# Delta-rule attention with a gated convolution: the 16-to-32 step in half as many products over 128 rows

## The chip, the cores and the metric

The kernel runs on one core of a Trainium2 chip. The metric is device microseconds of one execution. The core's engines have instruction queues of their own: TensorE (PE; its weight loads are listed as PEld), VectorE (DVE), ScalarE (ACT), GpSimd (POOL) and SyncE (SP). SP, ACT and POOL also issue DMA transfers (SPq, ACTq, POOLq).

## The reference

```python
def _attn_ref(q, k, v, beta) -> np.ndarray:
    B, H, S, D = q.shape          # 4, 8, 768, 48
    k_n = k / (np.linalg.norm(k, axis=-1, keepdims=True) + 1e-06)
    state = np.zeros((B, H, D, D), dtype=np.float32)
    y = np.zeros_like(q)
    for t in range(S):
        kt, vt, bt = (k_n[:, :, t], v[:, :, t], beta[:, :, t, None])
        y[:, :, t] = np.einsum('bhd,bhde->bhe', q[:, :, t], state)
        v_old = np.einsum('bhde,bhd->bhe', state, kt)
        state = state + bt[:, :, :, None] * np.einsum('bhd,bhe->bhde', kt, vt - v_old)
    return y.astype(np.float32)
```

Its output, 4 x 768 x 384, is the `x` of a gated convolution: `gate = sigmoid(conv of 5 taps over time)`, `out = (gate * (x @ w_val)) @ w_out`.

## The kernel before

**Tiling.** The 32 sequences (batch x head) are pairs: 16 pairs, one sequence in the upper and one in the lower 64 partitions. Time is cut into 12 chunks of 64 steps. Within a chunk the recurrence is solved as a triangular system; its inverse is built by doubling: blocks of 8 and 16 by small VectorE operations over all systems at once, then from 16 to 32 on TensorE (`m16`, `m32`), then from 32 to 64 (`lev1`, `lev2`). Two chunks make a group; the VectorE part runs once per group.

**A group's preparation.** `kq` (for the first group `kp` and `qp`) makes the Gram blocks of keys and queries; `kqevac` or `kpevac` takes them to GL on ScalarE, `kpfix` or the transfers `realign` shift half of the rows; `att` writes the masked query part. `trans_in` transposes to TL, `coef` and `newton` make the norms, `row`, `mergez8` and `merget8` the inverse of 16 x 16 blocks, `trans_out` writes them to XA (one half) and WB (the other). `gblocks` puts Gram blocks into G64 (transfer G<-GL), `wblocks` puts WB into W64: in group 0 by copies, later half by GpSimd copies and half by four transfers of SP (W<-WB). Per chunk, `m16` multiplies G64 with XA, `m16evac` takes it to YS, `m32` multiplies W64 with YS, `m32evac` takes it to XX; then `lev1`, `zevac`, `lev2`, `tevac`.

**A chunk's chain.** `e` (old state times keys), `eadd` on VectorE, `u`, `uevac`, `s` (new state, in SPS), `sevac`, and `y`; `stack` moves U and the masked part between halves of the partitions by transfers. `e` of the next chunk needs `sevac`.

**The convolution part.** Six segments of two chunks (the last cut in two): `conv`, `tap`, `sig`, `gate` on ScalarE and VectorE, `val` and `outp` on TensorE, `oevac`, and the store.

**Names in the trace of TensorE**: PB<-KQ is `kp`, `qp` or `kq`; PB<-XA,G `m16`; PB<-YS,W `m32`; PB<-XX,GL `lev1`; PB<-ZS,XX `lev2`; PB<-Y,KQ `e`; PB<-VT,XX `u`; SPS<-Y,KT and SPS<-US,KT `s`; PB<-KQ,Y `y`; PB<-X,WV `val`; PB<-WO,GT `outp`; SPS<-ZW `keep_warm`. Each product of the code is two instructions there.

**What sets the order.** Every operation is added to a plan with its reads and writes. The table ORDER is the order in which they are issued to the engines' queues; -1 in it is `keep_warm`, a product of zeros into an unused corner of SPS. BANKS gives each product group one of six PSUM banks. Each engine works its own part of ORDER strictly in turn.

The weights `w_val` and `w_out` come as double precision; `f64_0` to `f64_4`, `f64_low` and `f64_join` turn them into float32 on ScalarE, VectorE (lines 301 to 308) and GpSimd during the first third.

Of the kernel before, what the change touches and what calls it, by code (L numbers as in the profile page):

```python
# [16 lines left out]
C = 64  # L17
NCH = S // C
NG = NCH // 2
NP = 16  # L20
# [124 lines left out]
def kernel(  # L145
# [412 lines left out]
    def m32evac(ch, h):  # L558
        copy(A, XX[ch % NXX][:, HB * h:HB * h + HB, 32 * h:32 * h + 32], bank["m32", ch, h][:, 0:HB * 32].rearrange("p (j x) -> p j x", x=32))
# [499 lines left out]
```

## Time and profile before

| | |
|---|---|
| median of 3 runs | 322.74 us (318.75 to 323.77) |
| profiled execution | 322.35 us, its span 320.6 us |
| mean granted TensorE clock | 0.89 of full |
| busy: PE / DVE / ACT / POOL | 84% / 65% / 52% / 34% |
| bytes moved by DMA | 37.81 MB, 118 GB/s in the mean |

Busy shares are means over stages with different limits; matmuls are pipelined, so the start of one group and the start of the next tell more than a group's length. The granted clock has two levels, 1 (2.4 GHz) and 0.5 (1.2 GHz); a value between is a mean over a stretch.

### The profile page before, as it was taken

The numbers are of one execution on the slowest core, as the hardware profiler recorded it, in microseconds if no ns is written. First come the engines' busy times: TensorE is split into PE (matmuls) and PEld (weight loads), VectorE is DVE, ScalarE is ACT, GpSimd is POOL, SyncE is SP. The second block draws the span as 40 slices with busy tenths as digits, with TensorE's granted clock in tenths as the row PEclk, the third lists the DMA queues.
The fourth block names the chain that finished last, engine by engine and source line by source line (L and its number), as shares of the span: only waits on it lengthen the run. The fifth ranks groups of instructions, "written<-read, shape, count | busy, mean of one in ns | idle before, by whom it ended". The sixth has DMA issues, their size and how long they took to land.

```text
span 320.6 us, 16289 instructions
## 1 busy us (share of the span) xinstructions
PE 269.2 (84%) x7226; PEld 196.3 (61%) x7226; DVE 208.5 (65%) x461; ACT 166.0 (52%) x424; POOL 109.6 (34%) x255
## 2 busy tenths in 40 slices
PE   8204876688898988889897999698999997999996
PEld 4204865678654766567675565566665674766874
DVE  7989656598764879947737549756548800853580
ACT  3550457655447564468356384444276454576341
POOL 7313745448208527063262055180441140000000
PEclk9655597796679999999898999799999998999999
DMA  6999817833154748416763319564154132011123
GB/s 194 246 210 200 260 30 186 219 58 89 39 100 100 208 134 182 87 31 160 185 156 86 82 53 216 115 186 110 21 163 126 30 91 79 4 27 39 59 78 76
DMA packets 51398, 37.81 MB, mean 118 GB/s; under 512 B 33216, under 2 KB 44992, under 8 KB 51328
## 3 DMA queue, kind: packets, MB, share of 16 engines
q1 hardware_dynamic: 43392, 20.77, 27.6%
q0 software_dynamic: 4480, 13.64, 16.3%
q10 hardware_dynamic: 3456, 2.36, 3.2%
q8 instruction: 57, 0.93, 1.3%
q14 instruction: 13, 0.11, 0.1%
HBM read 22.92 MB, written 4.72 MB: 86 GB/s over the span
## 4 chain that ended last, share of the span: by engine, by line
PE 58%; DMA 11%; DVE 9%; ACT 7%; SPq 6%; issue 5%; ACTq 2%; POOL 2%; DVEq 0%
PE PB L243 28%; PE PB L705 13%; PE PB L715 13%; SPq L230 6%; DMA Y<-US 3%; PE SPS L243 2%; DMA G<-GL 2%; ACT XX L222 2%; ACTq L227 2%; DMA W<-WB 2%; ACT Y L222 2%; PE SPS L969 2%; DMA KQ<-AQ 1%; DMA X<-YSB 1%; DVE TLP L472 1%
## 5 line engine op out<-in xcount | busy, mean ns | idle before, releaser
L697 DVE SCALAR_TENSOR_TENSOR GT<-X,CW,GT 128x512 f32<-128x512 f32 (+1 forms) x84 | 56.3, 692 | 29.1 <-ACT GT L222 27.9
L705 PE MATMUL PB<-X,WV 128*128 128x512 f32 (+1 forms) x126 | 59.9, 596 | 2.6 <-ACT Y L222 1.6
L222 ACT ACTIVATE XX<-PB 32x256 f32<-32x256 f32 (+2 forms) x96 | 39.2, 427 | 30.1 <-PE PB L243 29.1
L715 PE MATMUL PB<-WO,GT 128*128 128x384 f32 x144 | 51.9, 499 | 0.6 <-ACT OS L222 0.6
L243 PE MATMUL PB<-KQ 48*64 48x128 f32 (+1 forms) x896 | 36.6, 313 | 17.0 <-DMA KQ<-in_qr_dram 5.9
L243 PEld LDWEIGHTS PB<-KQ 48*64 48x64 f32 x896 | 31.0, 173 | 24.2 <-ACT X L299 5.9
L715 PEld LDWEIGHTS PB<-WO,GT 128*128 128x128 f32 x144 | 25.7, 190 | 15.9 <-ACT OS L222 1.4
L705 PEld LDWEIGHTS PB<-X,WV 128*128 128x128 f32 x126 | 22.9, 201 | 15.0 <-issue 10.3
L222 ACT ACTIVATE GL<-PB 128x256 f32<-128x256 f32 (+1 forms) x44 | 16.0, 402 | 29.0 <-PE PB L243 17.7
L243 PE MATMUL PB<-KQ,Y 112*48 112x64 f32 (+2 forms) x768 | 27.5, 233 | 3.0 <-DMA Y<-US 2.5
L243 PEld LDWEIGHTS PB<-KQ,Y 112*48 112x48 f32 (+2 forms) x768 | 25.1, 133 | 7.3 <-issue 3.2
L222 ACT ACTIVATE Y<-PB 64x192 f32<-64x192 f32 x48 | 14.9, 322 | 19.7 <-PE PB L243 11.7
L411 DVE TENSOR_TENSOR KQ<-PB,MASK 64x256 f32<-64x256 f32 (+1 forms) x44 | 19.3, 443 | 7.3 <-ACT GL L222 6.5
L222 ACT ACTIVATE Y<-SPS 64x384 f32<-64x384 f32 (+1 forms) x44 | 20.4, 480 | 6.0 <-PE SPS L243 4.1
L709 DVE TENSOR_TENSOR GT<-PB,GT 128x512 f32<-128x512 f32 (+1 forms) x21 | 12.5, 609 | 14.6 <-ACT GT L701 8.0
L643 DVE TENSOR_TENSOR VT<-PB,VT 128x384 f32<-128x384 f32 x22 | 11.8, 554 | 15.6 <-issue 6.8
L243 PEld LDWEIGHTS PB<-VT,XX 64*64 64x64 f32 x768 | 13.8, 141 | 11.5 <-ACT XX L222 4.2
L243 PE MATMUL PB<-VT,XX 64*64 64x48 f32 x768 | 15.5, 227 | 6.1 <-DVE VT L643 2.5
L222 ACT ACTIVATE OS<-PB 128x384 f32<-128x384 f32 x24 | 11.5, 488 | 14.8 <-PE PB L715 9.6
L243 PE MATMUL PB<-XA,G 64*64 64x16 f32 x768 | 16.1, 223 | 3.3 <-DMA G<-GL 3.0
L591 POOL TENSOR_TENSOR VT<-VT,NRM 128x768 f32<-128x768 f32 x12 | 17.9, 1496 | 2.7 <-DMA VT<-in_vt_dram 1.2
L233 POOL DMA_DIRECT2D KQ<-in_qr_dram x16 | 8.9, 560 | 28.0 <-PE PB L243 28.0
(111 smaller groups left out, 459.6 us busy)
## 6 DMA issues: line engine op xcount, KB each, us to landing
out_dram<-OS SPq DMA_DIRECT2D x20, 192.0 KB, 2.6
KQ<-in_kf_dram POOLq DMA_DIRECT2D x16, 224.0 KB, 4.6
KQ<-AQ SPq DMA_DIRECT2D x24, 128.0 KB, 3.8
VT<-in_vt_dram POOLq DMA_DIRECT2D x16, 192.0 KB, 4.2
KT<-in_kt_dram POOLq DMA_DIRECT2D x16, 192.0 KB, 3.6
Y<-US ACTq DMA_DIRECT2D x24, 96.0 KB, 3.4
KQ<-in_qr_dram POOLq DMA_DIRECT2D x8, 256.0 KB, 5.0
KQ<-in_kf_dram SPq DMA_DIRECT2D x8, 224.0 KB, 4.5
```

The costliest lines, as they stand in the source:

```text
L222: A.activation(out=out, in_=in_, func=AF.Copy, **kw)
L227: A.dma_start(out=dst, in_=src)
L230: SP.dma_start(out=dst, in_=src)
L233: G.dma_start(out=dst, in_=src)
L243: PE.matmul(p, lhsT, rhs, start=start, stop=stop, tile_position=(row, col), skip_group_check=True)
L411: V.tensor_tensor(out=AQ[ch % NAQ][:, u:u + n] if v is None else R[ch % NR][r, v, u:u + n], in0=p[r], in1=MASK[h][r].unsqueeze(1).to_broad ...
L591: G.tensor_tensor(out=v, in0=v, in1=n.unsqueeze(3).to_broadcast([128, 2, HB, D]), op=ALU.mult)
L643: V.tensor_tensor(out=v, in0=bank["e", ch, h][:, 0:HB * D], in1=v, op=ALU.add)
L697: V.scalar_tensor_tensor(out=g, in0=xseg(sg, m, k), scalar=CW[:, m, k:k + 1], in1=g, op0=ALU.mult, op1=ALU.add)
L705: PE.matmul(bank["val", sg, m][:, 0:n], WV[:, k, 128 * m:128 * m + 128], xseg(sg, k, 4), start=k == 0, stop=k == NKT - 1)
L709: V.tensor_tensor(out=g, in0=bank["val", sg, m][:, 0:B * n].rearrange("p (b t) -> p b t", t=n), in1=g, op=ALU.mult)
L715: PE.matmul(bank["out", sg, i][:, 0:DM], gseg(sg)[:, k, w * i:w * i + w, :].rearrange("p b t -> p (b t)"), WO[:, k, :], start=k == 0, stop ...
```

## The change

`m16` and `m32` used products of 64 rows: two pairs' halves, each 64 x 64, and 32 products per chunk and step. Now one product covers both halves, 128 rows, with the moving tile block-diagonal: XA2 and YS hold the two halves' blocks side by side and zeros elsewhere. A chunk has 16 products for `m16` (32 moving columns, 16 before) and 16 for `m32` (64 moving columns, 32 before), each 128 x 64, and one PSUM bank per step instead of two. `spread` copies XA into XA2, one half on ScalarE, one on GpSimd; `m16evac` writes 64 partitions of 256 elements instead of 128 of 128, and YS holds one chunk instead of two. `wblocks` is a copy in all groups, four on ScalarE and four on GpSimd. `kpfix` goes half to ScalarE. Keys load rows 0 to 47 and 64 to 111 without the 16 rows between, in two transfers by row half instead of by head half; queries, from chunk 4 on, also without padding. ORDER and BANKS are new; ORDER holds 37 `keep_warm` (18 before).

```diff
 ORDER = [
-    13, 19, 29, 6, 23, 17, 14, 15, 28, 153, 154, 155, 1, 159, 156, 157, 158, 16, 31, 36, 40, 42, 41, 0, 30, 43, 235,
+    33, 34, 12, 6, 20, 16, 158, 32, 31, 17, 18, 35, 26, 27, -1, 36, 159, 46, 50, 47, 51, 240, 1, 19, 160, 161, 52, 49,
...
     G64 = one([128, NU, C], "G64")
     W64 = one([128, NU, C], "W64")
+    W5 = W64.rearrange("p (c j a) x -> p c j a x", c=2, a=2)
...
+    XA2 = one([128, NU, 32], "XA2")
     WB = one([128, NU, 16], "WB")
-    YS = one([128, NU, 32], "YS")
+    YS = one([128, NYS * NP, 64], "YS")
+    YS5 = YS.rearrange("p (c j a) x -> p c j a x", c=NYS, a=2)
...
     def kpfix(ch, h, a):
 
         q = 64 * a + 32 * (1 - h)
-        V.tensor_copy(out=GL[ch // 2 % 2][q:q + 32, h, ch % 2, :, 32 * h:32 * h + 32],
-                      in_=bank["kp", ch, h][q:q + 32].rearrange("p (j x) -> p j x", x=C)[:, :, 32 - 32 * h:64 - 32 * h])
+        copy(V if a else A, GL[ch // 2 % 2][q:q + 32, h, ch % 2, :, 32 * h:32 * h + 32],
+             bank["kp", ch, h][q:q + 32].rearrange("p (j x) -> p j x", x=C)[:, :, 32 - 32 * h:64 - 32 * h])
...
     def wblocks(g, q, h):
-        u, x, r = slice(NP * h, NP * h + NP), q % 64 + 16, (q + 64 * h) % 128
-        if g and h == 0:
-            load(W64[r + 16:r + 32, u, x:x + 16], WB[q + 16:q + 32, u])
-        else:
-            copy(G if h else A, W64[r:r + 32, u, x:x + 16], WB[q:q + 32, u])
+        x, a, r = q % 64 + 16, q // 64, q % 64 + 64 * h
+        t = WB.rearrange("p (h c j) x -> p h c j x", h=2, c=2)[:, h]
+        copy(G if h else A, W5[r:r + 32, :, :, a, x:x + 16], t[q:q + 32])
+
+    def spread(a):
+        r = slice(64 * a, 64 * a + 64)
+        copy(G if a else A, XA2[r, :, 16 * a:16 * a + 16], XA[r])
...
     def l_m16(ch, h):
-        p = bank["m16", ch, h]
-        for pp in range(HB * h, HB * h + HB):
-            for r in (0, 64):
-                to = 64 - r if h else r
-                yield p[to:to + 64, 16 * (pp % HB):16 * (pp % HB) + 16], G64[r:r + 64, unit(ch, pp), :], XA[r:r + 64, unit(ch, pp), :], r, to
+        p = bank["m16", ch]
+        for j in range(HB):
+            x = unit(ch, HB * h + j)
+            yield p[64 * h:64 * h + 64, 32 * j:32 * j + 32], G64[:, x, :], XA2[:, x, :], 0, 64 * h
...
     def m16evac(ch, h):
-        copy(A, YS.rearrange("p (h c j) x -> p h c j x", h=2, c=2)[:, h, ch % 2, :, 0:16],
-             bank["m16", ch, h][:, 0:HB * 16].rearrange("p (j x) -> p j x", x=16))
-
-    def l_m32(ch, h):
-        p = bank["m32", ch, h]
-        for pp in range(HB * h, HB * h + HB):
-            for r in (0, 64):
-                to = 64 - r if h else r
-                yield p[to:to + 64, 32 * (pp % HB):32 * (pp % HB) + 32], W64[r:r + 64, unit(ch, pp), :], YS[r:r + 64, unit(ch, pp), :], r, to
+        r, x = slice(64 * h, 64 * h + 64), 32 * h
+        copy(A, YS5[r, ch % NYS, :, :, x:x + 16].rearrange("p j a x -> p (j a) x"),
+             bank["m16", ch][r, 0:HB * 32].rearrange("p (s x) -> p s x", x=16))
+
+    def l_m32(ch, a):
+        p = bank["m32", ch]
+        for j in range(HB):
+            yield p[64 * a:64 * a + 64, C * j:C * j + C], W5[:, ch % 2, j, a, :], YS5[:, ch % NYS, j, a, :], 0, 64 * a
...
     def load_k(ch):
-        for h in range(2):
-            fetch(KF[ch % NKF][0:112, HB * h:HB * h + HB], kf[ch, :, HB * h:HB * h + HB], ch, [("KF", ch % NKF, h)], "LKF")
+        for f in range(2):
+            fetch(KF[ch % NKF][64 * f:64 * f + D], kf[ch, 64 * f:64 * f + D], ch, [("KF", ch % NKF, f)], "LKF")
 
     def load_q(ch):
         for v in range(2):
-            to = slice(0, 64) if v else slice(64, 112)
-            fetch(R[ch % NR][to, v], qr[ch, 1 - v, 0:to.stop - to.start], ch, [("R", ch % NR, "Q", v)], "LQR")
+            n = D if v == 0 or ch >= NR else C
+            to = 64 - 64 * v
+            fetch(R[ch % NR][to:to + n, v], qr[ch, 1 - v, 0:n], ch, [("R", ch % NR, "Q", v)], "LQR")
...
+        for a in range(2):
+            add("POOL" if a else "ACT", spread, (a,), r=["XA", "XA2z"], w=[("XA2", a)])
         for q in range(0, 128, 32):
             for h in range(2):
-                add("POOL" if h else "SP" if g else "ACT", wblocks, (g, q, h), r=["WB", "W64z"], w=[("W64", q, h)])
+                add("POOL" if h else "ACT", wblocks, (g, q, h), r=["WB", "W64z"], w=[("W64", q, h)])
```

The new ORDER at three places. First VectorE in the preparation of group 0, at the steps `row(5)` to the first of `mergez8`. L498 and L501 are the two steps of `row` (new: L503, L506), L308 and L301 steps of the weight conversion, L508 is `mergez8` (new: L513), L414 in the new order a mask (`att0`). Before:

```order
L498 TENSOR_TENSOR PR_85<-TT__84,TLP 128x100
L501 TENSOR_REDUCE TT__84<-PR_85 128x4x5
L498 TENSOR_TENSOR PR_85<-TT__84,TLP 128x144
L501 TENSOR_REDUCE TT__84<-PR_85 128x4x6
L308 TENSOR_SCALAR XX_79<-XX_79 128x384
L498 TENSOR_TENSOR PR_85<-TT__84,TLP 128x196
L301 TENSOR_SCALAR X_92<-X_92 128x384
L501 TENSOR_REDUCE TT__84<-PR_85 128x4x7
L508 TENSOR_TENSOR PR_86<-TLP,TT__84 128x128
```

Now:

```order
L503 TENSOR_TENSOR PR_85<-TT__84,TLP 128x100
L506 TENSOR_REDUCE TT__84<-PR_85 128x4x5
L503 TENSOR_TENSOR PR_85<-TT__84,TLP 128x144
L506 TENSOR_REDUCE TT__84<-PR_85 128x4x6
L414 TENSOR_TENSOR AQ_69<-PB_121,MASK_114 128x512
L503 TENSOR_TENSOR PR_85<-TT__84,TLP 128x196
L506 TENSOR_REDUCE TT__84<-PR_85 128x4x7
L513 TENSOR_TENSOR PR_85<-TLP,TT__84 128x256
```

The conversions have left this chain, and a mask of the second chunk has come in.

Second, SP's queue between the last G blocks of group 2 and the `realign` transfers of group 3 (GL<-GL); X<-YSB places `y` for the convolution, KQ<-AQ is the masked part. Before:

```order
L230 DMA X_92<-YSB_94 16x4x128 x4
L230 DMA W_75<-WB 16x16x16 x2
L230 DMA X_92<-YSB_94 16x4x128
L230 DMA W_75<-WB 16x16x16 x2
L230 DMA X_92<-YSB_94 16x4x128
L230 DMA KQ<-AQ_68 64x512
L230 DMA GL_73<-GL_73 32x16x32 x4
```

Now:

```order
L233 DMA G_74<-GL_72 16x32x16
L233 DMA X_93<-YSB_95 16x4x128 x5
L233 DMA KQ<-AQ_68 64x512
L233 DMA X_93<-YSB_95 16x4x128
L233 DMA KQ<-AQ_68 64x512
L233 DMA GL_73<-GL_73 32x16x32
```

The four W transfers are gone; the X transfers stay ahead of `realign`.

Third, ScalarE at the same group, around the evacuations of `m16` (YS<-PB). Before:

```order
L222 ACTIVATE OS_97<-PB_123 128x384
L222 ACTIVATE YS<-PB_124 128x8x16
L222 ACTIVATE YS<-PB_122 128x8x16
L222 ACTIVATE GT_96<-X_92,CW 128x512
L222 ACTIVATE YS<-PB_121 128x8x16
L222 ACTIVATE GL_73<-PB_124 128x256
```

Now:

```order
L225 ACTIVATE XA_89<-XA 64x32x16
L225 ACTIVATE GL_73<-PB_122 128x256
L225 ACTIVATE W_75<-WB 32x16x16 x3
L225 ACTIVATE YS<-PB_123 64x16x16
L225 ACTIVATE W_75<-WB 32x16x16
L225 ACTIVATE YS<-PB_123 64x16x16
L225 ACTIVATE GL_73<-PB_122 128x256
```

`spread` (XA_89<-XA) and four W copies have come in ahead of and between the evacuations of the first `m16`.

On TensorE, counted in the new ORDER: one `keep_warm` ahead of `kp`, 13 more before `m16` of chunk 2, one between there and the last output product, and 22 behind it (before: none, none, nine and nine). `kq` of chunk 2 and the first of chunk 3 stand ahead of the first `m16`; before, only one `kq` did.

## Rows read from the trace of the kernel before

**Rows 1.** Page, part 1: busy us, share of the span, instructions.

```profile
PE 269.2 (84%) x7226; PEld 196.3 (61%) x7226; DVE 208.5 (65%) x461; ACT 166.0 (52%) x424; POOL 109.6 (34%) x255
```

**Rows 2.** Windows: start:end us, length, busy us per engine, mean clock, DMA, GB/s.

```profile
74.40:93.70 19.30, 17.86 (x409) 13.27 (x401) 13.09 (x23) 8.01 (x23) 7.22 (x13) 0.65 0.30 61
93.70:139.20 45.50, 38.82 (x1250) 28.04 (x1250) 36.46 (x73) 26.51 (x69) 20.65 (x46) 1.00 0.55 133
...
234.90:277.90 43.00, 40.87 (x1084) 27.40 (x1083) 22.59 (x52) 23.59 (x60) 7.80 (x14) 0.96 0.30 85
277.90:316.20 38.30, 38.30 (x550) 26.75 (x549) 20.48 (x42) 20.09 (x52) 0.00 (x0) 1.00 0.18 49
316.20:320.60 4.40, 2.00 (x18) 1.80 (x17) 0.00 (x0) 0.49 (x1) 0.00 (x0) 1.00 0.36 87
```

**Rows 3.** Timeline of PE, 104 to 112 us: start, us, operation, idle before.

```profile
105.18 2.00 PE L243 MATMUL PB<-KQ,Y 112*48 112x64 f32 x64
107.11 1.15 PE L243 MATMUL PB<-Y,KQ 48*64 48x48 f32 x64
108.18 2.20 PE L715 MATMUL PB<-WO,GT 128*128 128x384 f32 x6
110.32 1.15 PE L243 MATMUL PB<-VT,XX 64*64 64x48 f32 x64
```

**Rows 4.** Timeline of PE, 256.8 to 267 us, the last `m16` and `m32`.

```profile
257.88 1.12 PE L243 MATMUL PB<-XA,G 64*64 64x16 f32 x64
258.93 2.20 PE L715 MATMUL PB<-WO,GT 128*128 128x384 f32 x6
...
264.25 2.07 PE L243 MATMUL PB<-YS,W 64*64 64x32 f32 x128
266.25 0.49 PE L969 MATMUL SPS<-ZW 128*128 128x128 f32 x2
```

**Rows 5.** Timeline of PE, 32 to 52 us.

```profile
32.73 2.15 PE L243 MATMUL PB<-XA,G 64*64 64x16 f32 x66 [2.96 <-DMA G<-GL]
...
40.24 1.56 PE L243 MATMUL PB<-YS,W 64*64 64x32 f32 x64
...
50.45 1.54 PE L243 MATMUL PB<-VT,XX 64*64 64x48 f32 x64 [2.40 <-POOL WV L315]
```

**Rows 6.** Timeline of DVE, 14 to 31 us.

```profile
19.30 0.36 DVE L301 TENSOR_SCALAR XX<-XX 128x384 f32<-128x384 f32 x1 [0.35 <-ACT XX L299]
...
23.33 1.17 DVE L301 TENSOR_SCALAR X<-X 128x384 f32<-128x384 f32 x1
...
30.02 1.03 DVE L529 STREAM_TRANSPOSE XA<-TT__84 128x512 f32<-128x512 f32 x1
```

**Rows 7.** Timeline of DVE, 50 to 62 us: `trans_in(1)` and `eadd(1)`.

```profile
50.89 1.95 DVE L472 STREAM_TRANSPOSE TLP<-GL 128x1024 f32<-128x1024 f32 x1 [1.62 <-DMA GL<-GL]
...
60.56 1.02 DVE L643 TENSOR_TENSOR VT<-PB,VT 128x384 f32<-128x384 f32 x2
```

**Rows 8.** Timeline of PE, 120 to 140 us: `m32(4)`.

```profile
130.30 1.45 PE L243 MATMUL PB<-YS,W 64*64 64x32 f32 x64 [1.13 <-DMA W<-WB]
```

**Rows 9.** Chain that ended last, in order of time: start, us, what.

```profile
25.23 7.36 DMA G<-GL
...
124.70 5.47 DMA W<-WB
...
310.38 5.81 PE PB L715 x18
316.19 2.01 PE SPS L969 x18
```

**Rows 10.** Groups by form, ACT: busy us, mean ns, idle before.

```profile
L222 ACT ACTIVATE YS<-PB 128x128 f32<-128x128 f32 x24 | 5.5, 275 | 10.8 <-PE PB L243 10.7
L222 ACT ACTIVATE G<-EYE 32x512 f32<-32x512 f32 x4 | 2.5, 622 | 0.1
L222 ACT ACTIVATE W<-WB 32x256 f32<-32x256 f32 x4 | 1.7, 414 | 0.1
```

More of the change, by code (lines that the diff above doesn't have):

```diff
@@ L40 @@
 ORDER = [
[70 rows of a table removed]
[71 rows of a table added]
 ]
 BANKS = (
-    "01234523304141500442511020300534334323130110105431405055345202510011041420301131321042332214511141053452133555"
-    "45532224313053154303513525103104253352541511124543243543444221043412240152103330525553324535313140114041423320"
-    "252414321331502"
+    "23014510000022325023435224012240141050343453245311325410222231131044101142535042321331244501111122215053522301"
+    "12430523403545203330510102425142405053524154231552402020333304052131030351451524220203400252521241350"
 )
@@ L169, in tiles @@
         return [one(shape, f"{name}{i}") for i in range(n)]
-    NKF, NR, NKTB, NVT, NAQ, NXX, NOS = 4, 4, 3, 3, 2, 4, 3
+    NKF, NR, NKTB, NVT, NAQ, NXX, NOS, NYS = 4, 4, 3, 3, 2, 4, 3, 1
     KQ = one([128, (NKF + 2 * NR) * NP * C], "KQ")
@@ L189 @@
     TT_ = one([128, 1056], "TT_")
-    PR = tiles(2, [128, 512], "PR")
+    PR = [one([128, 512 - 256 * i], f"PR{i}") for i in range(2)]
     ZT = one([128, 128], "ZT")
     XA = one([128, NU, 16], "XA")
+    XA2 = one([128, NU, 32], "XA2")
     WB = one([128, NU, 16], "WB")
-    YS = one([128, NU, 32], "YS")
+    YS = one([128, NYS * NP, 64], "YS")
+    YS5 = YS.rearrange("p (c j a) x -> p c j a x", c=NYS, a=2)
     XB = tiles(NX, [128, NKT, B, 2 * C + 4], "X")
@@ L558, in m32evac @@
     def m32evac(ch, h):
-        copy(A, XX[ch % NXX][:, HB * h:HB * h + HB, 32 * h:32 * h + 32], bank["m32", ch, h][:, 0:HB * 32].rearrange("p (j x) -> p j x", x=32))
+        copy(A, XX[ch % NXX][:, HB * h:HB * h + HB, 32 * h:32 * h + 32],
+             bank["m32", ch].rearrange("p (j h x) -> p j h x", h=2, x=32)[:, :, h])
     def l_lev(ch, h, n):
@@ L728 @@
             add("ACT", const_eye, (t[:, :, x:x + 16], 0, 16, r), r=["EYE"], w=[n + "z"])
-    add("ACT", const_eye, (YS[:, :, 16:32], 16, 16), r=["EYE"], w=["YSc"])
+    add("POOL", fill, (G, (XA2, 0.0)), w=["XA2z"], kind="zXA2")
+    add("POOL", fill, (G, (YS, 0.0)), w=["YSc"], kind="zYS")
+    for h in range(2):
+        r = slice(64 * h, 64 * h + 64)
+        add("ACT", const_eye, (YS[:, :, 32 * h + 16:32 * h + 32], 16, 16, r), r=["EYE"], w=["YSc"])
     add("ACT", const_eye, (ZS[:, :, 32:64], 0, 32), r=["EYE"], w=["ZSc"])
@@ L744 @@
     add("SP", load, (BE, beta), w=["BE"], kind="LB")
-    first = [("first", q) for q in range(0, 128, 32)]
     def load_k(ch):
-        for h in range(2):
-            fetch(KF[ch % NKF][0:112, HB * h:HB * h + HB], kf[ch, :, HB * h:HB * h + HB], ch, [("KF", ch % NKF, h)], "LKF")
+        for f in range(2):
+            fetch(KF[ch % NKF][64 * f:64 * f + D], kf[ch, 64 * f:64 * f + D], ch, [("KF", ch % NKF, f)], "LKF")
     def load_q(ch):
         for v in range(2):
-            to = slice(0, 64) if v else slice(64, 112)
-            fetch(R[ch % NR][to, v], qr[ch, 1 - v, 0:to.stop - to.start], ch, [("R", ch % NR, "Q", v)], "LQR")
+            n = D if v == 0 or ch >= NR else C
+            to = 64 - 64 * v
+            fetch(R[ch % NR][to:to + n, v], qr[ch, 1 - v, 0:n], ch, [("R", ch % NR, "Q", v)], "LQR")
     def q_of(ch):
@@ L782, in grams @@
                     for a in range(2):
-                        add("DVE", kpfix, (ch, h, a), r=[toks[h], *w], w=[("GD", gb, h, a, ch)], give=[toks[h]])
+                        add("DVE" if a else "ACT", kpfix, (ch, h, a), r=[toks[h], *w], w=[("GD", gb, h, a, ch)], give=[toks[h]])
             for ch in (2 * g, 2 * g + 1):
@@ L821, in prep @@
         for q in range(0, 128, 32):
-            add("SP", gblocks, (g, q), r=gl(0) + gl(1) + ["G64z"], w=[("G64", q)] + ([] if g else [("first", q)]))
+            add("SP", gblocks, (g, q), r=gl(0) + gl(1) + ["G64z"], w=[("G64", q)])
         plan_coef()
@@ L842, in prep @@
             x = ch % NXX
-            t1, t2 = ([(n, ch, h) for h in range(2)] for n in ("m16", "m32"))
-            add("PE", m16, (ch,), r=[("G64", q) for q in range(0, 128, 32)] + ["G64z", "XA"], w=t1, take=t1)
+            t1, t2 = ("m16", ch), ("m32", ch)
+            add("PE", m16, (ch,), r=[("G64", q) for q in range(0, 128, 32)] + ["G64z"] + [("XA2", a) for a in range(2)], w=[t1], take=[t1])
             for h in range(2):
-                add("ACT", m16evac, (ch, h), r=[t1[h]], w=[("YS", c, h)], give=[t1[h]])
-            add("PE", m32, (ch,), r=[("W64", q, h) for q in range(0, 128, 32) for h in range(2)] + ["W64z", "YSc"] + [("YS", c, h) for h in range(2)],
-                w=t2, take=t2)
+                add("ACT", m16evac, (ch, h), r=[t1, "YSc"], w=[("YS", ch % NYS, h)], give=[t1])
+            add("PE", m32, (ch,), r=[("W64", q, h) for q in range(0, 128, 32) for h in range(2)] + ["W64z", "YSc"] + [("YS", ch % NYS, h) for h in range(2)],
+                w=[t2], take=[t2])
             for h in range(2):
-                add("ACT", m32evac, (ch, h), r=[t2[h], ("XXz", x)], w=[("XX", x, "late", h)] + [("XX", x, h, a) for a in range(2)], give=[t2[h]])
+                add("ACT", m32evac, (ch, h), r=[t2, ("XXz", x)], w=[("XX", x, "late", h)] + [("XX", x, h, a) for a in range(2)], give=[t2])
             t1, t2 = ("lev", ch, 1), ("lev", ch, 2)
```

139 rows, old and new, of the table ORDER are left out of this document.

## Prediction

> **What bounds the kernel now.** I read the page first: TensorE is busy 84% of the span and no other engine comes near that [rows 1]. That share is a mean, so the second view is the busy time by stretch, with borders that I put at events of the work [rows 2]. From 93.70 on TensorE is busy 85% to 100% of every stretch, and from 277.90 to the last output product at 316.20 it never stops. Before 93.70 it is slow rather than idle: in 74.40 to 93.70 it is busy 17.86 of 19.30 us, but at a mean granted clock of 0.65. The clock has two levels, 1.2 and 2.4 GHz, so 70% of that stretch was at the lower one, and the lower one doubles a product's time: some 6.8 us of the 19.3.
>
> The third view is TensorE's timeline, read by the starts of neighbours, because durations overlap. At 2.4 GHz two `y` take 107.11 - 105.18 = 1.93 us, one `e` 1.07, one `u` 1.07 [rows 3], one `m16` 1.05, two `m32` 2.00 [rows 4]. A change of the tile's shape also costs: three output products in a row take 5.81 / 3 = 1.94 us each [rows 9], one that follows a product of another shape takes 110.32 - 108.18 = 2.14 [rows 3], so the switch is 0.20 us. With such unit costs and the order of the instructions, TensorE's work up to the last output product adds up to about 227 us of the 316; the other 89 us are waits and half clock. Two thirds of them lie ahead of chunk 3, where TensorE waits for VectorE's chain of small operations and for transfers. That is where an order can gain; behind it, only fewer or shorter products can.
>
> **Products.** The change takes 16 products of each kind per chunk where there were 32. Each trace product is two instructions, so 64 `m16` instructions become 32, and 64 `m32` become 32. The price of a new one is that of the nearest row, `y`: also 128 rows, also two halves of the output side by side, 64 moving columns, 1.93 / 64 = 30 ns an instruction. The old ones ran four at a time, at 1.05 / 64 = 16 ns. So half as many at twice the price: 32 x 30 ns = 0.97 us against 1.00 to 1.05. That gains 0.03 to 0.08 us for each of 24 steps, some 1 us in all. The bounds: `m16` moves 32 columns, not 64; if moving columns set its pace it costs half of `y`, and 12 of them give back another 6 us. If the weights set the pace (64 columns here, 48 in `y`), it is 30 x 64 / 48 = 40 ns, 1.29 us a step, a loss of 6 to 7 us over 24. I take the row itself, -1.
>
> Switches: `m16` and `m32` now share a shape with `y` alone. Counted in the order from `m16` of chunk 2 to the last output product, without the keep-warm products, there are 123 switches for 117, at 0.14 to 0.20 us: +1. One keep-warm product stands in this stretch where nine stood, at 2.01 / 9 = 0.22 us each [rows 9] and now and then a switch: -2. TensorE's work in the dense part: -2 together.
>
> **The prologue.** VectorE's chain decides: `trans_in(0)`, coefficients, `row`, merges, `trans_out`. Before, six weight conversions stand inside it, the first at 19.30 with 0.36 us, the longest at 23.33 with 1.17, 3.1 us together [rows 6]; now they stand behind both `trans_out`. In their place stand two masks that stood behind, and the WB transpose (1.03 like XA's) goes ahead of XA's; together that is about as long. XA is then ready within a microsecond of the 31.05 of before [rows 6]. The copy of XA into XA2, half on ScalarE, half on GpSimd, comes on top: 64 partitions of 512 elements, by the 32x512 copy 0.62 us [rows 10]. But before, the first `m16` did not wait for XA: it waited for the last G block, 25.23 + 7.36 = 32.59 [rows 9], and that transfer still stands behind the second chunk's mask. So `m16` starts at 32 to 33.5 as before: 0. Keys without padding rows, and queries from chunk 4 on, are 96 rows where there were 112, a seventh less; nothing on the chain waits for them behind the first microseconds: 0.
>
> **Chunks 0 to 2.** Here the order matters. Before, two `m16` at half clock (66 instructions in 2.15 us) and two `kq` stand between 32.73 and `m32(0)` at 40.24; one more `kq` follows [rows 5]. Now three of these four `kq` are ahead of `m16(0)`, in time that TensorE spends waiting, and `m32(0)` follows after one `m16` and one `kq`: two times about 2 us, so near 37, 3.5 us earlier; `u(0)` from 50.45 to about 46. The Gram blocks of chunks 2 and 3 are out 4 to 5 us earlier, so `trans_in(1)`, at 50.89 [rows 7], starts near 45. From it to the end of `eadd(1)` before were 61.58 - 50.89 = 10.7 us [rows 7]; now three more `row` steps (1.4 us) and up to four conversions (1.6) stand ahead of `eadd(1)`: 13.7, so 58.5 for 61.6. The rest of the chain to XA of group 1 has those rows already behind it. The lead at `m16(2)` comes to 3 to 6 us; I take -4.5, with 0 (all conversions and the later `eadd` eat it) and -8 (the lead of `m32(2)`, whose W blocks no longer come by transfer) as bounds.
>
> **The W blocks.** In groups 1 to 5, half of W came by four transfers on SP's queue, behind X transfers of 0.6 us each. At group 2 the last of them took 5.47 us [rows 9] and `m32(4)` started at 130.30 after a wait of 1.13 for it [rows 8], with another idle microsecond ahead. Now ScalarE copies them: four at 0.414 us [rows 10], ready about 3 us after the transpose. Gain -2 there; later groups show no such wait, and TensorE has other products to run. What stood behind those transfers on SP, the `realign` transfers of the next group, moves up too. Bounds 0 and -5.
>
> **What ScalarE gets.** Per group: four copies of 0.41, one `spread` of 0.62, and per chunk two evacuations of 256 elements where two of 128 took 0.275; by the copies of 256 that is +0.3 [rows 10]. That is 2.9 us per group, 14 in five groups, on an engine busy 52%. In the dense part it lies beside TensorE's work; the `spread` is on the way from XA to `m16` in groups 1 and 2. I take +1, bounds 0 and +6.
>
> **The clock.** Fourteen keep-warm products now stand ahead of `m16(2)`, thirteen of them from `u(0)` on or right before it, where TensorE waits. If they hold the clock at 2.4 GHz through 74 to 94 us, up to 6.8 us come back. The trace does not show a keep-warm product there, so I take a quarter, -1.5.
>
> **The end.** After the last output product 22 keep-warm products follow, before 9. They took 2.01 us for 18 instructions [rows 9], so 22 take 4.9. The span ended 4.40 us after that product [rows 2], with the store. Now TensorE ends later than the store: +1.
>
> Sum against the profiled execution (322.35 us, span 320.6, so 1.75 around it; the median of the runs is 0.4 higher, which I leave out): 322.35 - 2 - 4.5 - 2 + 1 - 1.5 + 1 = 314.35. Since every wait removed ahead of 94 us may partly return as a wait for VectorE, which was busy 36.46 of 45.50 us in the next stretch [rows 2], I add a little under 1: **315 us**.
>
> **Rivals.** *The lead is eaten* (the wait that takes the place of the others): VectorE and ScalarE, with the same work or more, set the pace from 94 to 175, and the dense part then starts where it did. For it: VectorE's 80% there. Left are 322.35 - 2 + 1 + 1: 322, or 320 if a part is kept. *The clock holds* from chunk 0 on: 315 - 5 = about 309, for it the many keep-warm products, against it that the mean clock was below 1 in 234.90 to 277.90 too, amid dense work [rows 2]. *The 128-row products are slow* (the side beyond no change): if the weights of one half cannot load while the other half's product runs, a new pair costs its 30 ns and a load in the open. An old load cost at most 16 ns with four at a time, so 66 alone and 33 for two side by side: 63 ns, 2.0 us a step, +1 us for 24 steps, of which some 20 lie on TensorE's path: 315 + 20 = 335. It decides from about 45 ns an instruction on. The row against it is `y`, whose loads of 48 columns hide at 30 ns. The Trainium skill, "TensorE: Matmul & The Clock Gate", Part 3 (The mechanism), speaks for it: a weight load overlaps a running matmul only where the row groups differ, and two 128-row tiles share all of them. By that rule the time would be the 335; the `y` row disagrees with it.
>
> **How the numbers follow.** Forecast 0.44, clock 0.20, lead eaten 0.27, slow products 0.09. The range 306 to 323 takes in the first three with the products' lower bound in part and leaves out the fourth and the rims. Within 2% (316.3 to 329.2, about what a measurement of this kernel can tell from no change): the lead-eaten case and a fifth of the forecast, 0.36; faster by more, 0.55; slower, 0.09.
>
> **What would show it.** In the changed profile: `m16` and `m32` of one chunk at 0.9 to 1.05 us from start to start at 2.4 GHz; `m16(0)` at 32 to 33.5; `u(0)` near 46, `m16(2)` near 70; no W transfers and no wait of `m32(4)`; a clock above 0.65 from 74 to 94; the last output product near 309, and keep-warm products that end last. I am wrong if the 128-row instructions take over 40 ns, or if `m16(2)` is not earlier than 74.

## The result, and the profile after

The changed kernel takes 303.1 us in the median (298.6 to 304.5), the kernel before 322.35 in the same call. The ratio is 0.936 (95% interval 0.916 to 0.955): 6.4% faster, where 315 us was forecast and the range ended at 306. Executions of one kernel lie some per cent apart, and the medians here take all of them, the ratios only the fast ones. The profiled execution of the changed kernel spans 302.2 us.

Of the page after, part 1, against [rows 1]:

```profile
PE 263.0 (87%) x6496; PEld 192.4 (64%) x6496; DVE 213.9 (71%) x457; ACT 184.0 (61%) x455; POOL 114.0 (38%) x263
```

The two kernels, cut at two events: the first `m16` of chunk 2 (or 3), and the end of the last output product. Windows of the kernel before (columns as in [rows 2]):

```profile
0.00:74.44 74.44, 44.58 (x1481) 38.90 (x1481) 58.67 (x148) 37.59 (x92) 35.70 (x96) 0.72 0.74 177
74.44:316.19 241.75, 222.59 (x5742) 155.59 (x5735) 149.83 (x314) 127.93 (x332) 73.92 (x160) 0.94 0.41 100
```

And of the changed kernel:

```profile
0.00:74.87 74.87, 50.34 (x1381) 43.04 (x1381) 60.68 (x144) 40.39 (x97) 37.76 (x97) 0.73 0.69 152
74.87:296.32 221.45, 207.72 (x5080) 144.61 (x5075) 153.26 (x313) 143.14 (x357) 76.27 (x167) 0.99 0.44 110
296.32:302.20 5.88, 4.91 (x44) 4.71 (x43) 0.00 (x0) 0.49 (x1) 0.00 (x0) 1.00 0.24 59
```

In these two profiles the first part is as long as before; in e8 and e14 below, which have the changed kernel's order, it is 2 us shorter (72.5). The gain is behind it: 241.75 - 221.45 = 20.3 us. TensorE's idle time there fell from 241.75 - 222.59 = 19.2 us to 13.7, its busy time by 14.9. Much of the latter is the clock: added up over windows of 2 us (length x 2 x (1 - clock)), TensorE ran 27.3 us at the lower level before and 3.4 after, and 23.9 us at half speed are at most 12 us of work. At least 3 us are left for products, switches and the fewer keep-warm products. These are shares of the busy time, not yet causes: e1 and e11 below have over 20 us of half clock again and keep most of the gain. Behind the last product 1.5 us came on top.

Windows after, two of them with the borders of [rows 2]:

```profile
74.40:93.70 19.30, 16.38 (x435) 11.36 (x427) 16.20 (x28) 14.04 (x32) 11.07 (x20) 1.00 0.65 158
93.70:139.20 45.50, 40.59 (x1122) 28.30 (x1124) 34.71 (x70) 29.28 (x77) 18.50 (x45) 0.96 0.55 126
```

The clock of the first was 0.65 before. Timeline of PE after, the products of chunks 6 and 7, against [rows 4]:

```profile
163.71 1.12 PE L246 MATMUL PB<-XA,G 128*64 128x32 f32 x32
164.76 1.10 PE L246 MATMUL PB<-KQ 48*64 48x128 f32 x32
...
170.03 1.15 PE L246 MATMUL PB<-YS,W 128*64 128x64 f32 x32
170.98 1.10 PE L246 MATMUL PB<-XA,G 128*64 128x32 f32 x32
172.02 1.13 PE L709 MATMUL PB<-X,WV 128*128 128x512 f32 x2
```

From start to start a `m16` takes 1.04 to 1.05 us with the switch behind it, a `m32` in front of a `m16` of the same shape 0.95: 30 ns an instruction, the price of `y`.

Groups by form of ScalarE after, against [rows 10]:

```profile
L225 ACT ACTIVATE W<-WB 32x256 f32<-32x256 f32 x24 | 9.9, 414 | 2.0 <-DVE WB L534 1.6
L225 ACT ACTIVATE YS<-PB 64x256 f32<-64x256 f32 x24 | 9.0, 376 | 2.6 <-PE PB L246 1.9 <-ACT XX L225 0.6
L225 ACT ACTIVATE XA<-XA 64x512 f32<-64x512 f32 x6 | 3.8, 630 | 4.7 <-DVE XA L534 4.6
```

### The profile page after: what moved, and what is told of

Its sections match the earlier page's. It is cut to its first block, busy times and chain, and to the rows that moved or that the text cites. A ratio compares the mean times of both kernels' runs of the same rounds, so it can differ in the third digit from the quotient of the medians.

```text
span 302.2 us, 14831 instructions
## 1 busy us (share of the span) xinstructions
PE 263.0 (87%) x6496; PEld 192.4 (64%) x6496; DVE 213.9 (71%) x457; ACT 184.0 (61%) x455; POOL 114.0 (38%) x263
## 4 chain that ended last, share of the span: by engine, by line
PE 50%; DVE 15%; DMA 14%; ACT 9%; issue 6%; POOL 3%; SPq 2%; ACTq 0%; POOLq 0%; DVEq 0%
PE PB L246 24%; PE PB L709 13%; PE PB L719 9%; DMA KQ<-in_qr_dram 5%; DMA XX<-in_w_val_dram 4%; DMA Y<-US 3%; ACT W L225 2%; PE SPS L978 2%; PE SPS L246 2%; SPq L233 2%; DVE GT L701 2%; DVE PR L525 2%; ACT XX L225 2%; DVE TLP L475 1%; DMA GL<-GL 1%
## 5 line engine op out<-in xcount | busy, mean ns | idle before, releaser
L701 DVE SCALAR_TENSOR_TENSOR GT<-X,CW,GT 128x512 f32<-128x512 f32 (+1 forms) x84 | 58.9, 724 | 13.5 <-ACT GT L225 12.1
L709 PE MATMUL PB<-X,WV 128*128 128x512 f32 (+1 forms) x126 | 56.7, 571 | 3.8 <-DMA GL<-GL 1.9
L246 PE MATMUL PB<-KQ 48*64 48x128 f32 (+1 forms) x896 | 34.5, 304 | 17.0 <-DMA KQ<-in_qr_dram 6.3
L225 ACT ACTIVATE XX<-PB 32x256 f32<-32x256 f32 (+2 forms) x96 | 39.2, 427 | 13.3 <-PE PB L246 10.4
L246 PEld LDWEIGHTS PB<-KQ 48*64 48x64 f32 x896 | 29.1, 166 | 20.7 <-issue 7.0
L246 PE MATMUL PB<-KQ,Y 128*48 128x64 f32 (+2 forms) x768 | 27.5, 227 | 1.7 <-issue 0.9
L246 PEld LDWEIGHTS PB<-KQ,Y 128*48 128x48 f32 (+2 forms) x768 | 24.6, 127 | 5.6 <-issue 3.2
L414 DVE TENSOR_TENSOR KQ<-PB,MASK 64x256 f32<-64x256 f32 (+1 forms) x44 | 19.1, 443 | 10.1 <-ACT GL L225 6.0
L225 ACT ACTIVATE Y<-SPS 48x384 f32<-48x384 f32 (+1 forms) x44 | 20.6, 480 | 9.2 <-PE SPS L246 7.2
L225 ACT ACTIVATE GL<-PB 128x256 f32<-128x256 f32 (+2 forms) x48 | 17.5, 396 | 8.1 <-DVE AQ L414 3.2
L225 ACT ACTIVATE Y<-PB 64x192 f32<-64x192 f32 x48 | 14.3, 320 | 13.1 <-issue 5.9
L246 PEld LDWEIGHTS PB<-VT,XX 64*64 64x64 f32 x768 | 12.7, 134 | 9.0 <-issue 5.5
L246 PE MATMUL PB<-YS,W 128*64 128x64 f32 x384 | 15.2, 233 | 1.9 <-ACT YS L225 0.9
```

What stands on the lines that cost most here:

```text
L225: A.activation(out=out, in_=in_, func=AF.Copy, **kw)
L246: PE.matmul(p, lhsT, rhs, start=start, stop=stop, tile_position=(row, col), skip_group_check=True)
L414: V.tensor_tensor(out=AQ[ch % NAQ][:, u:u + n] if v is None else R[ch % NR][r, v, u:u + n], in0=p[r], in1=MASK[h][r].unsqueeze(1).to_broad ...
L701: V.scalar_tensor_tensor(out=g, in0=xseg(sg, m, k), scalar=CW[:, m, k:k + 1], in1=g, op0=ALU.mult, op1=ALU.add)
L709: PE.matmul(bank["val", sg, m][:, 0:n], WV[:, k, 128 * m:128 * m + 128], xseg(sg, k, 4), start=k == 0, stop=k == NKT - 1)
```

## The experiments

Three theories stood at the start. A: the new order removes waits behind `m16` of chunk 2, and falls of the clock with them. B: the 13 keep-warm products hold the clock. C: the products, copies and loads gain by themselves, in any order. All times in one table; "stretch" runs from the first `m16` of chunk 2 or 3 to the end of the last output product, in the profiled execution, "idle" is the stretch less TensorE's busy time in it, "half" the time at the lower clock in it, added up over windows of at most 2 us.

| run | order behind chunk 2 | median us | ratio to before (95%) | stretch, idle, half |
|---|---|---|---|---|
| before | old | 322.4 | | 241.8, 19.2, 27.3 |
| after | new | 303.1 | 0.936 (0.916 to 0.955) | 221.5, 13.7, 3.4 |
| e1 no keep-warm in front | new | 301.7 | 0.939 (0.929 to 0.948) | 225.6, 11.1, 20.5 |
| e3 64 rows | new | 340.8 | 1.066 (1.056 to 1.077) | 250.3, 25.1, 47.8 |
| e4 before, 21 keep-warm more | old | 321.9 | 1.007 (0.998 to 1.016) | 234.2, 16.1, 10.3 |
| e5 products alone | old | 329.3 | 1.019 (1.008 to 1.029) | 242.9, 22.6, 25.7 |
| e6 W copies alone | old | 322.1 | 1.005 (1.001 to 1.010) | 245.4, 22.2, 34.1 |
| e7 W by transfers | new | 320.4 | 0.998 (0.993 to 1.002) | 244.9, 27.4, 30.8 |
| e8 padded loads | new | 302.3 | 0.942 (0.934 to 0.949) | 222.6, 14.3, 3.4 |
| e9 all but the order | old | 339.6 | 1.065 (1.056 to 1.074) | 253.0, 27.9, 36.5 |
| e10 new, then old | old | 332.9 | 1.045 (1.037 to 1.053) | 258.3, 33.1, 44.4 |
| e11 old, then new | new | 313.6 | no interval | 224.9, 9.7, 23.3 |
| e12 no keep-warm at all | new | 301.6 | 0.944 (0.937 to 0.951) | 224.9, 13.3, 13.7 |
| e13 two banks a step | new, 9 later | 322.7 | 1.010 (1.001 to 1.019) | 238.4, 23.1, 20.4 |
| e14 banks by turn | new | 302.8 | 0.951 (0.942 to 0.961) | 223.2, 14.9, 3.4 |
| e15 W transfers later | new | 316.6 | 0.991 (0.986 to 0.996) | 235.3, 25.4, 17.1 |
| e16 weights later | new | 302.5 | 0.943 (0.910 to 0.976) | 224.3, 14.3, 10.3 |

**Keep-warm products.** e1 takes 15 of them out of the changed kernel's ORDER, e12 all 37, e4 puts 21 into that of the kernel before (here 4 of them ahead of `e` of chunk 2, number 577):

```diff
 # e1
-    252, 246, 253, 238, 259, 168, 65, 361, 360, -1, 121, 119, 169, ...
+    252, 246, 253, 238, 259, 168, 65, 361, 360, 121, 119, 169, ...
 # e4
-    204, 466, 410, 379, 577, 579, ...
+    204, 466, 410, 379, -1, -1, -1, -1, 577, 579, ...
```

> The changed kernel without its 15 keep-warm products ahead of the last output product; the 22 behind it stay. Theory A (the order removes the waits behind 74 us, and the clock's falls go with them): 300 to 305 us, within 1% of the changed kernel, granted clock near 1.0 from 75 to 91 us as with them. Theory B (the 13 keep-warm products ahead of m16 of chunk 2 hold the clock there): 308 to 311 us, with a mean granted clock of about 0.65 from 75 to 94 us, as before the change.

> The kernel before with 21 keep-warm products more, where TensorE waits: 4 ahead of e of chunk 2, 4 ahead of lev1 of chunk 2, 5 ahead of val of segment 2 (second m), 8 ahead of the first y of chunk 7. If the half clock after those waits is what the old order lost (some 6.7 us at 75 to 94, 1.7 at 174 to 177, 2 at 205 to 209): 312 to 315 us, clock above 0.95 in those stretches. If VectorE and ScalarE set the pace there, or the clock falls all the same: 318 to 323 us.

> The changed kernel without any of its 37 keep-warm products. By the term for the end (22 products that end 1 to 1.5 us after the store would) and by the run without the 15 in front, which was as fast: 300 to 302 us. If the keep-warm products hold a clock that the profile of one run did not show: 306 us or more.

B falls. Without them TensorE does run 10 to 17 us longer at the lower level (in e1 the clock from 75 to 91 us was 0.84, not near 1 as expected), but the stretch grows by 3 to 4 us only, and the median does not grow. In e12 the span ends 4.5 us behind the last output product instead of 5.9. `m16` of chunk 2 starts at 72.6 there, but in e8 and e14, which keep the products, at 72.5, so this is not their doing. e4 shows less than it seems to: in its profile, of an execution of 316.5 us, 17 us of half clock are gone, but by the granted clock of all its executions (span x 2 x (1 - clock)) the mean is 64 us against 69 for the kernel before in the same call. The products hardly raised the clock there, and the median does not move.

**Undoing the order or the parts.** e2 and e9 have the change's code in the order of before, with spread right behind the transpose. e2 is not in the table: it kept `m16evac` of the odd chunk ahead of `m32` of the even one, so that YS for one chunk was overwritten and part of the chunks was computed from other data, and its half of `kpfix` on ScalarE stood behind the wait for the weights. It took 340.9 us. e9 mends both:

```diff
 # e9, ORDER of before in the numbers of the change: m32 of chunk 0 is 126, m16evac of chunk 1 is 139, 140
-    ... 197, 250, 138, 140, 139, 172, ...
+    ... 197, 250, 138, 172, ...
...
-    ... 204, 203, 126, 127, 266, ...
+    ... 204, 203, 126, 139, 140, 127, 266, ...
 # e9, kpfix
-        copy(V if a else A, GL[ch // 2 % 2][q:q + 32, ...
+        copy(V, GL[ch // 2 % 2][q:q + 32, ...
```

> All of the change except order, banks and keep-warm products: the operations stand as before the change, spread right behind XA's transpose. Theory A (order): 318 to 323 us, with the falls of the clock at 75, 157, 174 and 205 us still there. Theory C (the 128-row products, the W copies and the loads give the gain in any order): 303 to 310 us.

> The change without order, banks and keep-warm products: 128-row products, W copies and loads without padding in the order of before, kpfix on VectorE as before, the eight evacuations of m16 behind m32 as in the run of the products alone. Theory A (the new order is needed, and it needs these parts): 318 to 330 us. Theory C (the parts together gain without the order): 303 to 312 us.

e5 has the products alone in the old order, e6 the W copies alone in the kernel before:

```diff
 # e5: as e9, with the loads of before and
+        if g and h == 0:
+            load(W5[r + 16:r + 32, :, :, a, x:x + 16], t[q + 16:q + 32])
 # e6
-        if g and h == 0:
-            load(W64[r + 16:r + 32, u, x:x + 16], WB[q + 16:q + 32, u])
-        else:
+        if 1:
```

> The kernel before with the 128-row products alone: XA2 and spread, YS for one chunk, one bank a step; loads, W transfers, kpfix, keep-warm products and order as before, except that eight evacuations of m16 of an odd chunk stand behind m32 of the chunk before it, which YS for one chunk needs. Theory A (new order, with the banks that the products free for it): 318 to 328 us, no faster than before, since spread lies between XA and m16. Theory C (the products themselves gain): 305 to 314 us.

> The kernel before with all W blocks as copies, four of them on ScalarE where the transfers stood in the order. If the transfers' wait at m32 of chunk 4, and what they hold up on SP's queue, is a main part of the gain: 310 to 316 us. If not: 317 to 323 us.

C falls: neither the products nor the W copies gain alone, and all parts together lose 6.5%. e10 and e11 change the order at `m16` of chunk 2 (328 in the change's numbers): one list up to it, what is left in the other's order.

```diff
 # e10: new list ahead of 328, the rest of the old one behind
-    ... 328, 471, 685, 588, 329, 414, ...
+    ... 328, 329, 413, 330, 585, 233, ...
```

> The changed kernel's operations in the new order up to m16 of chunk 2, what is left in the order of before. If the gain comes from the order behind m16 of chunk 2, as the traces read (that product starts at 74.4 before and 74.9 after, and 20 us are gained behind it): 318 to 326 us, with half clock and waits behind 75 us again. If it comes from what the new order has done ahead of it: 302 to 308 us.

> The other way round: the order of before up to m16 of chunk 2 (kpfix on VectorE), what is left in the new order. If the gain comes from the order behind m16 of chunk 2: 300 to 310 us. If from what stands ahead of it: 318 to 326 us.

The stretches of e10 and e11 (windows, columns as in [rows 2]):

```profile
74.53:332.79 258.26, 225.18 (x5096) 156.55 (x5091) 148.51 (x314) 141.94 (x357) 78.14 (x168) 0.91 0.39 94
```

```profile
82.62:307.50 224.88, 215.14 (x5074) 151.61 (x5075) 151.79 (x310) 142.22 (x354) 73.36 (x157) 0.95 0.41 101
```

The table sorts itself by its second column: where all of the changed code stands in the new order behind chunk 2, the stretch is 221 to 226 us with 10 to 15 us idle, whatever the beginning, the keep-warm products, the loads or the bank table (after, e1, e8, e11, e12, e14, e16). In the old order it is 234 to 258. That is A as far as the order goes, but not the clock: in these seven runs half clock is anything from 3.4 to 23.3 us. e11, with nearly as much of it as before, has a stretch 17 us shorter, 9.4 us less idle and 7.5 less busy. But the new order with the old products, or with W by transfers, loses everything again (e3, e7).

Many sizes were missed. e2, e5, e9 and e10 were slower than the ranges given for A. e11's 313.6 us is above its range too; in its profile the old order takes 82.6 us up to `m16` of chunk 2. e3 came out where C was expected, at 314 us or more; e13 below explains about half of that.

**What the new order needs: banks.** e3 is the new order with the old products; where the two banks of a step were not free, nine operations stand later. e13 keeps the new products and takes the second bank:

```diff
 # e13
-        p = bank["m16", ch]
+        p = bank["m16", ch, h]
...
-            t1, t2 = ("m16", ch), ("m32", ch)
+            t1, t2 = [("m16", ch, h) for h in range(2)], ("m32", ch)
...
-                w=[t2], take=[t2])
+                w=[t2], take=[t2, ("m32b", ch)])
```

> The new order with the old products: 64 rows, 32 per chunk and step, two banks a step, no spread; W by copies and loads without padding as in the change. Nine operations stand later than in the new order, until banks are free. Theory A: 303 to 308 us (up to 0.1 us more for each of 24 steps, less by two spreads per group, and the nine). Theory C: 314 us or more.

> The changed kernel with its 128-row products, but two PSUM banks for each m16 and a second bank kept free for each m32, as the old products had; the same nine operations stand later as in the run with the old products in the new order, until banks are free. If the banks that the new products free are what the new order needs: 325 to 343 us, like that run (340.8). If the 64-row products themselves were slow there: 300 to 308 us.

> The changed kernel in its own order, each product group in the bank that has been free longest, instead of the table's (154 of 211 differ). If only the number of banks counts: 300 to 306 us. If the table's choice carries part of the gain: 310 us or more.

Timeline of PE in e13, `kq` of chunk 9 behind `m16` of chunk 6, and the next `m16`:

```profile
171.22 1.13 PE L245 MATMUL PB<-XA,G 128*64 128x32 f32 x32
172.27 0.43 PE L245 MATMUL PB<-KQ 48*64 48x128 f32 x2
175.54 1.55 PE L245 MATMUL PB<-KQ 48*64 48x128 f32 x30 [2.84 <-ACT YS L224]
...
183.90 0.25 PE L245 MATMUL PB<-XA,G 128*64 128x32 f32 x2
185.89 1.62 PE L245 MATMUL PB<-XA,G 128*64 128x32 f32 x30 [1.74 <-DVE AQ L413]
```

`kq` waits for a bank that the evacuation of `m16` (YS) gives back, `m16` of chunk 7 for one that a mask (AQ) reads. In the changed kernel neither waits (163.71 to 172.02 above). Two banks a step, with the nine later operations that they force, cost 322.7 - 303.1 = 19.6 us, the whole gain, though 322.7 is 2 us below the range expected; which bank the table picks costs nothing (e14). With the old products (e3) it is 18 us more than e13 in the median and 334.4 - 321.9 = 12.5 in the profiled executions. There half clock accounts for at most (47.8 - 20.4) / 2 = 13.7 us; why the clock was lower, and so what the old products cost by themselves in this order, stays open.

**What it needs: no W transfers on SP's queue.** e7 puts them back where the copies stand, e15 behind the last X transfer ahead of `m32` (769, 771, 773 and 775 are those of group 3):

```diff
 # e7 and e15
+        if g and h == 0:
+            load(W5[r + 16:r + 32, :, :, a, x:x + 16], t[q + 16:q + 32])
+        else:
-        copy(G if h else A, W5[r:r + 32, :, :, a, x:x + 16], t[q:q + 32])
+            copy(G if h else A, W5[r:r + 32, :, :, a, x:x + 16], t[q:q + 32])
 # e15, ORDER
-    ... 765, 769, 851, 855, 866, 775, ...
+    ... 862, 861, 864, 769, 775, 771, 773, 894, ...
```

> The changed kernel with half of the W blocks by four transfers per group again, in groups 1 to 5, at the place of the copies. If the copies are a main part of the gain: 307 to 315 us, TensorE waiting for W<-WB. If not: 300 to 306 us.

> The changed kernel with half of the W blocks by transfers again (groups 1 to 5), now on SP's queue behind the last X transfer ahead of m32, not in front of the X transfers. If what cost 18 us in the first such run was that W transfers, waiting for VectorE's transpose, held up X transfers whose data were ready: 301 to 308 us. If the transfers' own time at m32 costs it: 314 us or more.

Timeline of e7 at group 3, first ScalarE's last copy to YSB and VectorE's WB transpose, then SP's queue:

```profile
168.74 0.38 ACT L225 ACTIVATE YSB<-PB 112x256 f32<-112x256 f32 x1 [0.30 <-PE PB L246]
173.10 1.03 DVE L537 STREAM_TRANSPOSE WB<-TT__84 128x512 f32<-128x512 f32 x1
...
164.01 0.64 SPq L233 DMA_DIRECT2D G<-GL  x1
174.20 0.59 SPq L233 DMA_DIRECT2D W<-WB  x1
174.89 0.58 SPq L233 DMA_DIRECT2D X<-YSB  x1
175.57 2.54 SPq L233 DMA_DIRECT2D W<-WB  x2
178.20 1.22 SPq L233 DMA_DIRECT2D X<-YSB  x2
179.47 0.59 SPq L233 DMA_DIRECT2D W<-WB  x1
180.10 1.88 SPq L233 DMA_DIRECT2D X<-YSB  x3
```

The same place after:

```profile
157.88 0.39 ACT L225 ACTIVATE YSB<-PB 112x256 f32<-112x256 f32 x1 [0.30 <-PE PB L246]
...
158.32 4.44 SPq L233 DMA_DIRECT2D X<-YSB  x6
165.65 0.51 SPq L233 DMA_DIRECT2D KQ<-AQ  x1
```

In the changed kernel the six X transfers start as soon as YSB is written, at 158.3 us, and are issued by 162.8. In e7, which is already 11 us behind, YSB is written at 169.1, but the first W transfer waits for the WB transpose until 174.1, and the X transfers are issued from 174.9 to 182. Counted from the copy to YSB, that is 6 to 9 us later than in the changed kernel. The waits of PE in e7 and in e15 (line, waited for: us in total, times, longest):

```profile
PE PB L712 <- DMA X<-YSB: 10.9, 3, 6.1
```

```profile
PE PB L246 <- DMA W<-WB: 15.3, 5, 6.6
```

Behind the X transfers the W transfers are late for `m32` instead. So e15 gets back only 320.4 - 316.6 = 3.8 of e7's 17.3 us (e7 had been expected at 307 to 315), and its expectation of 301 to 308 failed: one queue in strict order can't serve both, in either order that was tried.

**Loads, and the prologue.** e8 loads the padding rows again, e16 moves two weight conversions of ScalarE (184 and 179, `f64_low` and `f64_0`) behind the W copies of group 0:

```diff
 # e8
-        for f in range(2):
-            fetch(KF[ch % NKF][64 * f:64 * f + D], kf[ch, 64 * f:64 * f + D], ...
+        for h in range(2):
+            fetch(KF[ch % NKF][0:112, HB * h:HB * h + HB], kf[ch, :, HB * h:HB * h + HB], ...
 # e16
-    ... 103, 101, 184, 104, 105, 106, 179, 108, ...
+    ... 103, 101, 104, 105, 106, 108, ...
...
-    ... 360, -1, 121, 119, 169, ...
+    ... 360, -1, 121, 119, 184, 179, 169, ...
```

> The changed kernel with keys and queries loaded with the padding rows again. By the prediction's zero: 300 to 305 us. If the smaller loads end waits in the dense part: 306 us or more.

> The changed kernel with two conversion steps of the weights on ScalarE (f64_low and f64_0 of the first block, which wait for the weights' transfer until 29.1 us) moved behind the copies of W for group 0. If that wait is why XA is ready at 34.8 us and not at 31: XA by 33 us or earlier and m16 of chunk 0 1.5 to 3 us earlier. If a lead is carried to the end: 299 to 301 us; if VectorE eats it before m16 of chunk 2: 302 to 304 us.

The chain of waits after, in order of time (start, us, what), shows what e16 was to remove:

```profile
17.83 11.24 DMA XX<-in_w_val_dram
...
29.09 0.55 ACT WV L314
29.64 0.43 ACT XX L302
...
32.17 0.39 ACT GL L225
...
32.58 0.42 DVE AQ L414
33.01 0.94 DVE WB L534
33.95 0.87 DVE XA L534
```

A mask of VectorE stands ahead of both transposes, it waits for ScalarE's GL copy, and that stood behind the weights' transfer. In e16 XA is ready at 33.7 us, 1.1 earlier than after, not 1.8 or more, and `m16` of chunk 0 starts 0.7 earlier, not 1.5 to 3; nothing of that is to be seen in the time (302.5 and 303.1). But e8 and e14, which leave these steps where they are, have XA at 32.7 and 33.1, so e16 shows no effect at all. In it the mask starts at 31.4 us, behind 1.4 us of idle for which the profile shows no reason. The loads are worth nothing that could be measured, as forecast.

## Why the prediction was wrong

**The step that failed** is the last sentence of its first part: "That is where an order can gain; behind it, only fewer or shorter products can." All of the gain in the profile came behind it, and all but some 2 us of it in e8 and e14. The prediction had counted 89 us of waits and half clock and put two thirds of them ahead of chunk 3. The other third was on the table too: 19.2 us idle and 27.3 us of half clock from 74 us on. It priced an order there at -2 for one wait of `m32` and -1.5 for the clock; the order, with the banks and the queue that it needs, changed the stretch by 20.

**W blocks**: -2 was the price of the wait shown in [rows 8]. Alone in the old order the copies brought nothing (e6). In the new order they are worth 17 us (e7), because they leave SP's queue to transfers that are ready, and because W is not late for `m32`, as it is in e15. "TensorE has other products to run" held for the old order; the X transfers that feed those products are what the queue delays.

**One bank a step** was in the text on the change, and no term priced it. By e13 it is worth the whole gain; the waits shown there are of `kq` and of the next `m16`, for banks that an evacuation or a mask still holds.

**The terms were added as if they were independent.** Measured one by one they come to +6 us by the ratio (e5) and 0 to +3 (e6), all parts without the order to +21 (e9), and with it to -21. No run that lacks one of the three, the order, the freed bank or the copies, is more than 1% faster than before.

**The clock**: -1.5, at most -6.8, against at most 12 us in the profile. But the rival "the clock holds", as the prediction meant it, is not the answer: without a single keep-warm product the kernel is as fast (e12). Part of the half clock costs nothing: e12 has 10.3 us more of it than e14, 5.1 us of work, and a stretch 1.7 us longer; TensorE is idle 1.6 us less.

**Products**: right. 30 ns an instruction, as `y`; the slow-products rival is out. The rule that spoke for it, that a weight load overlaps a running matmul only where the row groups differ (the Trainium skill, "TensorE: Matmul & The Clock Gate", Part 3, The mechanism), does not show in these rows: 128-row tiles side by side run at 30 ns.

**Prologue**: 0 was too good. `m16` of chunk 0 started at 35.97 instead of 32 to 33.5. The weights' transfer is issued later (17.83, before 12.29), and ScalarE waits for it ahead of the GL copy. It lands at 29.07 in this profile; in e15, e8 and e14 at 26.2, 27.0 and 27.3, and `m16` starts at 33.4, 33.9 and 34.2. That the wait is the cause is not shown, as e16 gains nothing by leaving it out.

**Chunks 0 to 2**: -4.5 was within its bounds but too much: `u(0)` at 48.25 (forecast 46, before 50.45), `m16` of chunk 2 at 74.87, no lead left (2 us in e8 and e14). That step failed on VectorE, as the rival "the lead is eaten" said, only that the dense part didn't care. `trans_in(1)` did start near 45, but XA of group 1 ends at 72.96, as before (72.85). From `trans_in(1)` to XA after:

```profile
45.61 1.96 DVE L475 STREAM_TRANSPOSE TLP<-GL 128x1024 f32<-128x1024 f32 x1 [0.17 <-issue]
...
55.59 1.58 DVE L494 TENSOR_TENSOR TLP<-TLP,CT 128x256 f32<-128x256 f32 x1
...
61.76 2.49 DVE L503 TENSOR_TENSOR PR<-TT__84,TLP 128x196 f32<-128x196 f32 x1
...
71.90 1.06 DVE L534 STREAM_TRANSPOSE XA<-TT__84 128x512 f32<-128x512 f32 x1
```

The rows of 1.58 and 2.49 us take 0.42 and 0.35 elsewhere (in the prologue after: 20.01 and 23.93); beside them stand eight steps of the conversion, 3.2 us.

**The end**: +1 was 1.5 (5.88 - 4.40 us behind the last product).

## What to carry to other kernels

A change that frees a bank or a queue slot is worth what the order can do with it; price it by what waits for that bank or queue in every stage, not by the wait that the old order shows. Parts that need one another have no prices that can be added. Where an order is written anew, idle time amid dense work is as open to it as that at the start. A transfer whose source isn't ready, standing on a queue ahead of transfers whose data are, holds these up (e7).

## What the runs showed of the hardware

VectorE's operation with two inputs stood still beside GpSimd's. Timeline of POOL after, at the row of 2.49 us above:

```profile
61.57 1.01 POOL L318 TENSOR_TENSOR WV<-WV,X 128x384 f32<-128x384 f32 x1
62.54 1.48 POOL L595 TENSOR_TENSOR VT<-VT,NRM 128x768 f32<-128x768 f32 x1
```

GpSimd started at 61.57, VectorE's product at 61.76 ended at 64.25, right behind the second of the two, 2.1 us late; in the ten other runs with this pair the same row took 2.48 or 2.49, and in e11, where GpSimd has nothing beside it, 0.36. The Trainium skill, "SBUF — State Buffer", section "SBUF: two separate sides", states such an exclusive lock between a VectorE operation with two SBUF inputs and a GpSimd operation that reads SBUF. The trace agrees; here the loser waited for two operations in a row.

The clock did not fall behind every wait: in the changed kernel a pause of 2.12 us at 85.0 was followed by full clock, one of 1.92 at 128.4 by some 3.4 us at half. In e14 the pause at the first of these places, 2.51 us, was followed by half clock.
